# Windowed attention inside a two-layer MoE kernel: scores as 64x64 products in the visit of the values products, and a new order of each mixed step

## The chip, the core and the metric

The kernel runs on one core of a Trainium2 chip. The metric is the device time of one execution in microseconds, median of three. The core has five engines, each with its own in-order queue: TensorE (PE in the profile, its weight loads PEld), VectorE (DVE), ScalarE (ACT), GpSimd (POOL) and SyncE (SP, which here only issues DMAs). Matrix products land in PSUM, which has eight banks of 2 KB per partition; everything else lives in SBUF.

## What is computed

Three stages, one after the other. Attention over 4 batches, 8 heads, 576 positions and 64 channels, each query seeing the 64 positions that end at its own; then a dense MLP on 2304 tokens (512 to 2048 and back) with an activation called mish in the kernel; then a top-1 mixture of 8 experts.

```python
def _attn_ref(q, k, v):                       # [4, 8, 576, 64]
    scores = np.matmul(q, k.transpose(0, 1, 3, 2)) / np.sqrt(64)
    rel = pos[:, None] - pos[None, :]
    scores = np.where((rel >= 0) & (rel < 64), scores, -1000000000.0)
    attn = np.exp(scores - scores.max(-1, keepdims=True))
    return np.matmul(attn / (attn.sum(-1, keepdims=True) + 1e-09), v)

h = x @ w_in                                   # x: [2304, 512]
g = h * np.tanh(np.log1p(np.exp(h)))           # plain h above 20
x = g @ w_out
# each token: expert argmax(logits), out = prob * (relu(x @ w1[e]) @ w2[e])
```

## The kernel before

**Attention** goes by steps `a` of 64 queries (36 of them, two to a group `g`). A step's scores are four 128x128 tiles, one for each pair `c` of heads: rows are 2 heads x 64 queries, columns are 128 keys. `scores` (L150) first puts the mask into the bank by an identity product (L161, steps below `MASK_PE` = 26), then multiplies (L163) the keys by `qd`, a copy of the queries with zeros where the head and the channel half don't belong together; `qd` is cleared once (L107, L108) and filled by two DMAs per group (L139). `largest` (L172) takes the row maximum: below step 26 one reduction on VectorE (L178) and a scaling on GpSimd (L180), from step 26 on a fused mask-and-maximum on VectorE (L186). `exps` (L198) are four exponentials on ScalarE (L204), `inverse` and `scale` (L218, L228) normalise on GpSimd, `flip` (L235) transposes on TensorE (L241), `flipped` (L246) copies the transposed tile `t` to SBUF as `pt`, `values` (L249) multiplies with v (L257, eight 64x64 products), and `done` (L262) copies the result `o` out (L274) and, every second step, issues the store of x on ScalarE's queue (L277). `t` and `o` take turns in one PSUM bank, `s` has a bank of its own.

**Order.** Twelve attention steps run alone (`att_alone`, L1306). Then 28 mixed steps `i` follow, in which attention step and MLP step are woven together, with `na = 12 + i`. A mixed step is: 12 hidden products of MLP step `i` (L386 to L388, one weight load each, 512 columns), `att_a` (L1269), 12 output products of MLP step `i - 2` (L444 to L446; none in steps 0 and 1), `att_b` (L1291). So TensorE visits attention twice per step: scores of `na - 1` and flip of `na - 3` in `att_a`, values of `na - 3` in `att_b`. All engines run in exactly the order in which these Python functions issue.

**Woven in on VectorE and ScalarE**: mish in five ScalarE operations (L503 to L506, L514) and three VectorE operations (L508, L515, L516), the split of its result into a rounded part `g` and a rest (L522 on ScalarE, L523 on VectorE), and the conversion of 32 pieces of float64 weights, each three integer operations on VectorE (L330, L334, L338: the parts that `convert_start` counts), a cast on ScalarE (L356) and a subtraction on VectorE (L1252). The conversion is spread over the alone steps and the mixed steps 0 to 13, six or five parts a step (`CONV` = 3 in each half, one less in the second half of every third step).

After mixed step 27 the MLP goes on without attention, and then the routing and the experts.

Of the kernel before, what the change touches and what calls it, by code (L numbers as in the profile page):

```python
# [11 lines left out]
F32 = mybir.dt.float32  # L12
# [5 lines left out]
AF = mybir.ActivationFunctionType  # L18
# [23 lines left out]
PT_ACT = range(5, 28)  # L42
# [4 lines left out]
CONV = 3  # L47
# [42 lines left out]
class Attention:  # L90


    def __init__(self, nc, ctx, tc, qT, kT, v, x_dram, consts, spare, first_x):
        self.nc, self.qT, self.kT, self.v, self.x = nc, qT, kT, v, x_dram
        self.c = consts
# [3 lines left out]
        self.px = pool("att_x", 1)  # L99
# [3 lines left out]
        self.spare, self.first_x = spare, first_x  # L103
        self.qd = []
        for i in range(2):
            t = self.pq.tile([P, KD, 2, BLK * 2], F32, name=f"qd{i}")
            nc.vector.memset(t[0:64, :, 1], 0.0)  # L107
            nc.vector.memset(t[64:128, :, 0], 0.0)  # L108
            self.qd.append(t)
# [19 lines left out]
        self.kt, self.v_in, self.held = {}, {}, None  # L129
        self.s, self.p, self.t, self.o = {}, {}, {}, {}  # L130

    def load(self, g):
        nc = self.nc
        qd = self.qd[g % 2]
# [15 lines left out]
    def scores(self, a):  # L150
        nc = self.nc
        g, j = divmod(a, 2)
        if a % 2 and a < PRE:
            s = self.spare.tile([P, KD, P], F32, name="s_acc", tag="acc1")
        else:
            s = self.ps.tile([P, KD, P], F32, name="s")
        masked = a < MASK_PE
        if masked:
            mask = self.c["mask0_b"] if a % (S // BLK) == 0 else self.c["mask_b"]
            mask = mask.unsqueeze(1).broadcast_to([P, KD, P])  # L160
            nc.tensor.matmul(s, self.eye, mask, start=True, stop=False)  # L161
        for c in range(KD):
            nc.tensor.matmul(  # L163
                s[:, c, :],
                self.qd[g % 2][:, c].rearrange("p h (q j) -> p j (h q)", j=2)[:, j],
                self.kt[g][:, c, j * BLK : j * BLK + P],
                start=not masked,
                stop=not masked or c == KD - 1,
            )
        self.s[a] = s  # L170

    def largest(self, a, scaled_by=None):  # L172

        nc = self.nc
        s = self.s.pop(a)
        mx = self.pp.tile([P, KD], F32, name="mx")
        if a < MASK_PE:
            nc.vector.tensor_reduce(out=mx, in_=s, op=ALU.max, axis=AX.X)  # L178
            by = scaled_by or nc.gpsimd
            by.tensor_scalar(mx, mx, -1.0 / math.sqrt(HD), None, ALU.mult)  # L180
            self.p[a] = s, mx, 1.0 / math.sqrt(HD)
            return
        p = self.pp.tile([P, KD, P], F32, name="p")
        mask = self.c["mask0"] if a % (S // BLK) == 0 else self.c["mask"]
        for c in range(KD):
            nc.vector.tensor_tensor_reduce(  # L186
                out=p[:, c, :],
                in0=s[:, c, :],
                in1=mask,
                scale=-1.0 / math.sqrt(HD),  # L190
                scalar=3.0e38,
                op0=ALU.add,
                op1=ALU.min,
                accum_out=mx[:, c : c + 1],
            )
        self.p[a] = p, mx, -1.0

    def exps(self, a, alone=False):  # L198
# [4 lines left out]
        for c in range(KD):  # L203
            nc.scalar.activation(  # L204
                p[:, c, :],
                s[:, c, :],
# [26 lines left out]
    def flip(self, a):  # L233
        nc = self.nc
        p, _ = self.p.pop(a)  # L235
        if a < PRE - LT:
# [11 lines left out]

    def values(self, a):  # L249
# [3 lines left out]
        o = self.ps.tile([P, KD, BLK], F32, name="o", tag="to")  # L253
        for c in range(KD):
            for hh in (slice(0, 64), slice(64, 128)):
                d = slice(c * P + hh.start, c * P + hh.stop)
                nc.tensor.matmul(  # L257
                    o[hh, c, :], self.v_in[g][j][:, d], pt[:, c, hh], start=True, stop=True
                )
        self.o[a] = o  # L260

    def done(self, a):  # L262
# [11 lines left out]
        nc.scalar.copy(xs[:, :, j * BLK : (j + 1) * BLK], o)  # L274
# [23 lines left out]
class Rounds:  # L298
# [199 lines left out]
    def mish_a(self, h):  # L498

        nc = self.nc  # L500
        y = self.m_pool.tile([P, 2 * G], F32, name="y")
        r = self.m1_pool.tile([P, 2 * G], F32, name="r")
        nc.scalar.activation(y, h, AF.Tanh, scale=0.5)  # L503
        nc.scalar.activation(y, y, AF.Square, scale=-0.5, bias=self.c["half"][:, 0:1])  # L504
        nc.scalar.activation(r, y, AF.Exp, scale=SEED_B)
        nc.scalar.activation(r, r, AF.Copy, scale=SEED_A, bias=SEED_C)  # L506
        p = self.m1_pool.tile([P, 2 * G], F32, name="pq")
        nc.vector.scalar_tensor_tensor(p, y, 1.0, r, ALU.add, ALU.mult)  # L508
        return y, r, p, h

    def mish_b(self, y, r, p, h):
# [4 lines left out]
        nc.vector.scalar_tensor_tensor(y, p, -0.5, h, ALU.add, ALU.mult)  # L516
# [667 lines left out]
def tile_kernel(tc, a):  # L1184
    nc = tc.nc
    with ExitStack() as ctx:
# [22 lines left out]
        with tc.manual_schedule():  # L1209
# [4 lines left out]
            A = Attention(nc, att_ctx, tc, a["qT"], a["kT"], a["v"], a["x"], c, R.acc_ps, R.first_x)  # L1214
# [32 lines left out]

            def convert_end():
                def low():
                    while low_parts:  # L1250
                        key, args = low_parts.pop(0)
                        nc.vector.tensor_tensor(*args)  # L1252
                        ready.add(key)

                low()
# [488 lines left out]
```

## Time and profile before

| | |
|---|---|
| median of 3 runs | 722.13 us (721.99 to 722.43) |
| the profiled execution, its own time | 722.25 us |
| its span, first to last instruction | 720.5 us |
| TensorE busy | 699.2 us, 97% |
| VectorE busy | 539.2 us, 75% |
| ScalarE busy | 475.0 us, 66% |
| GpSimd busy | 152.2 us, 21% |
| chain that ended last | PE 81%, DVE 7%, ACT 4%, DMA 3%, issue 3% |

The span is what the trace covers; 1.75 us of the execution's own time lie around it. "Busy" is time with at least one instruction under way, over the whole span. The chain is the sequence of waits and instructions followed back from the last one. A matmul's duration is from its start to its end in the pipeline; what one costs in a row of them is the distance from its start to the next start. Products on float32 leave two records each (the mask and the 512-column products one).

### The profile page before, as it was taken

The numbers are of one execution on the slowest core, as the hardware profiler recorded it, in microseconds if no ns is written. First come the engines' busy times: TensorE is split into PE (matmuls) and PEld (weight loads), VectorE is DVE, ScalarE is ACT, GpSimd is POOL, SyncE is SP. The second block draws the span as 40 slices with busy tenths as digits, with TensorE's granted clock in tenths as the row PEclk, the third lists the DMA queues.
The fourth block names the chain that finished last, engine by engine and source line by source line (L and its number), as shares of the span: only waits on it lengthen the run. The fifth ranks groups of instructions, "written<-read, shape, count | busy, mean of one in ns | idle before, by whom it ended". The sixth has DMA issues, their size and how long they took to land.

```text
span 720.5 us, 11849 instructions
## 1 busy us (share of the span) xinstructions
PE 699.2 (97%) x4061; PEld 581.2 (81%) x4061; DVE 539.2 (75%) x1349; ACT 475.0 (66%) x1021; POOL 152.2 (21%) x290
## 2 busy tenths in 40 slices
PE   6879999999999999999999999999999999999996
PEld 5668877888888888888888888998888888888885
DVE  4889998976555479999999998699898754333361
ACT  4989888899777678776787677777454023342382
POOL 5753233332322010101101011401012305010031
PEclk9999999999999999999999999999999999999999
DMA  8996666752231332000000000732144604322340
GB/s 262 300 264 212 220 203 226 220 164 82 81 96 29 106 102 89 30 1 30 31 1 30 1 31 15 249 118 88 60 146 164 217 0 140 125 95 97 117 177 33
DMA packets 48615, 83.76 MB, mean 116 GB/s; under 512 B 3937, under 2 KB 23393, under 8 KB 48418
## 3 DMA queue, kind: packets, MB, share of 16 engines
q1 hardware_dynamic: 36578, 64.40, 28.7%
q0 software_dynamic: 4432, 14.46, 5.6%
q10 hardware_dynamic: 7536, 4.06, 2.0%
q8 instruction: 34, 0.56, 0.3%
q14 instruction: 35, 0.29, 0.1%
HBM read 69.78 MB, written 13.19 MB: 115 GB/s over the span
## 4 chain that ended last, share of the span: by engine, by line
PE 81%; DVE 7%; ACT 4%; DMA 3%; issue 3%; POOL 0%; SPq 0%; POOLq 0%; ACTq 0%
PE acc L444 11%; PE acc L446 11%; PE acc L445 11%; PE h L386 11%; PE h L388 11%; PE h L387 11%; PE s L163 3%; DMA qd<-qT 2%; PE o L257 2%; ACT p L204 1%; PE t L241 1%; PE h L374 1%; PE h L373 1%; PE h L370 1%; DVE cv L338 1%
## 5 line engine op out<-in xcount | busy, mean ns | idle before, releaser
L444 PE MATMUL acc<-w,g 128*128 128x512 f32 x256 | 102.8, 401 | 0.0
L653 DVE CUSTOM_DVE_ANT_0 junk<-row,wg 128x512 bf16<-128x512 f32 x144 | 99.1, 689 | 2.6
L446 PE MATMUL acc<-w,g 128*128 128x512 f32 x256 | 100.1, 391 | 0.0
L445 PE MATMUL acc<-w,g 128*128 128x512 f32 x256 | 99.8, 390 | 0.0
L530 ACT ACTIVATE g<-h 128x512 fp32r<-128x512 f32 x32 | 19.1, 598 | 112.0 <-PE h L388 111.2
L503 ACT ACTIVATE y<-h 128x512 f32<-128x512 f32 x72 | 43.0, 598 | 56.0 <-PE h L388 48.7
L231 POOL TENSOR_SCALAR p<-p,r 128x128 f32<-128x128 f32 x144 | 65.8, 473 | 65.5 <-DVE r L224 62.4
L386 PE MATMUL h<-xw,w 128*128 128x512 f32 x192 | 76.3, 398 | 0.0
L388 PE MATMUL h<-xw,w 128*128 128x512 f32 x192 | 75.0, 391 | 0.0
L387 PE MATMUL h<-xw,w 128*128 128x512 f32 x192 | 74.9, 390 | 0.0
L732 POOL DMA_INDIRECT xs_dram<-row,posi x18 | 20.0, 1111 | 228.2 <-DVE pq L515 83.7
L508 DVE SCALAR_TENSOR_TENSOR pq<-y,r 128x512 f32<-128x512 f32 x72 | 49.6, 689 | 24.3 <-ACT r L506 20.2
L514 ACT ACTIVATE pq<-pq,mid 128x512 f32<-128x512 f32 x72 | 52.4, 727 | 17.3 <-DVE pq L508 12.5
L531 DVE SCALAR_TENSOR_TENSOR g<-h,g 128x512 fp32r<-128x512 f32 x32 | 22.1, 690 | 55.0 <-ACT g L530 51.8
L523 DVE TENSOR_TENSOR g<-y,g 128x512 fp32r<-128x512 f32 x72 | 49.5, 687 | 17.8 <-ACT g L522 17.8
L515 DVE SCALAR_TENSOR_TENSOR pq<-pq,r 128x512 f32<-128x512 f32 x72 | 50.1, 696 | 13.4 <-ACT pq L514 11.5
L446 PEld LDWEIGHTS acc<-w,g 128*128 128x128 f32 x256 | 48.1, 188 | 10.6
L445 PEld LDWEIGHTS acc<-w,g 128*128 128x128 f32 x256 | 48.3, 189 | 9.2
L444 PEld LDWEIGHTS acc<-w,g 128*128 128x128 f32 x256 | 48.2, 188 | 9.0
L504 ACT ACTIVATE y<-y,half 128x512 f32<-128x512 f32 x72 | 52.2, 725 | 2.3
L516 DVE SCALAR_TENSOR_TENSOR y<-pq,h 128x512 f32<-128x512 f32 x72 | 49.5, 687 | 2.9
L444 PE MATMUL acc<-ew,g 128*128 128x512 f32 x128 | 50.8, 397 | 0.0
(296 smaller groups left out, 1782.4 us busy)
## 6 DMA issues: line engine op xcount, KB each, us to landing
s<-e_w SPq DMA_DIRECT2D x20, 1024.0 KB, 6.1
v<-v SPq DMA_DIRECT2D x36, 256.0 KB, 4.1
raw<-w_in SPq DMA_DIRECT2D x16, 512.0 KB, 5.0
raw<-w_out SPq DMA_DIRECT2D x16, 512.0 KB, 4.1
kt<-kT SPq DMA_DIRECT2D x17, 384.0 KB, 5.5
qd<-qT SPq DMA_DIRECT2D x36, 128.0 KB, 5.2
x_dram<-xs ACTq DMA_DIRECT2D x14, 256.0 KB, 3.2
xraw<-x_dram SPq DMA_DIRECT2D x10, 256.0 KB, 3.5
```

The lines of the kernel that those rows point to most:

```text
L231: nc.gpsimd.tensor_scalar(p[:, c, :], p[:, c, :], r[:, c : c + 1], 0.0, ALU.mult, ALU.add)
L386: nc.tensor.matmul(h, w[:, 0, k, fs], xh, start=(k == 0), stop=False)
L387: nc.tensor.matmul(h, w[:, 0, k, fs], xl, start=False, stop=False)
L388: nc.tensor.matmul(h, w[:, 1, k, fs], xh, start=False, stop=(k == KD - 1))
L444: nc.tensor.matmul(acc[c], gc[:, 0], w[:, 0, f], start=first, stop=False)
L445: nc.tensor.matmul(acc[c], gc[:, 0], w[:, 1, f], start=False, stop=False)
L446: nc.tensor.matmul(acc[c], gc[:, 1], w[:, 0, f], start=False, stop=last)
L504: nc.scalar.activation(y, y, AF.Square, scale=-0.5, bias=self.c["half"][:, 0:1])
L508: nc.vector.scalar_tensor_tensor(p, y, 1.0, r, ALU.add, ALU.mult)
L514: nc.scalar.activation(p, p, AF.Square, bias=self.c["mid"][:, 0:1])
L515: nc.vector.scalar_tensor_tensor(p, p, 0.75, r, ALU.add, ALU.mult)
L653: nc.vector.tensor_tensor_reduce(out=junk, in0=rows[c][:, 0:D], in1=self.wg[:, e], scale=1.0, scalar=0.0, op0=ALU.mult, op1=ALU.add, accum ...
```

## The change

- The queries are loaded as they are (`qt`, one DMA per group, 64 channels of one head of a pair on the lower and of the other on the upper 64 partitions), without zeros and without the clearing. Scores become eight products per step of 64 channels, 64 queries and 128 keys, ordered so that four successive ones use the four 64x64 quarters of the array; the mask becomes four products of 64x256. The row halves write to different banks: half 0 to the bank `xo` that `o` also uses (`s0`, columns 256 to 511), half 1 to the bank `s` (`s1`).
- In the mixed steps the scores of `na` (not of `na - 1`) are issued directly before the values of `na - 3`, so `att_a`'s visit keeps only the flip.
- `t`, `o` and one half of the scores now share one bank, so the flip must wait until the maximum, the exponentials (steps below 26) and the copy of `o` have read `xo`. Readers of `xo` on different engines are made to wait for one another (`one_at_a_time`).
- The maximum is two reductions, one for each bank, and its scaling in the mixed steps goes from GpSimd to VectorE (`shift`).
- Two tables, `ORDER_A` and `ORDER_B`, set each mixed step's order; mish is cut into parts that they name. The conversion parts are 6, 2, 5 and 3 in steps 0 to 3, six in each of steps 4 to 13, and the last three in step 14.
- The x tile `xs` gets a second buffer, and mixed step 0 copies `pt` on VectorE.

```diff
-PT_ACT = range(5, 28)
+PT_ACT = *range(5, 12), *range(13, 28)
-CONV = 3
+ORDER_A = {
...
+    None: ("done", "max 0", "high", "conv 1", "nm", "low", "conv 1", "scale", "y1", "conv 1", "y2", "fetch", "exps", "flip"),
+}
...
+for i in range(3):
+    n = 3
+    ORDER_B[i] = ("tanh", "pt", "mish", "high", "conv 1", "low", "conv 1", "pq", "conv 1", "scores", "max 1 next", "values", "g")
...
-        self.px = pool("att_x", 1)
+        self.px = pool("att_x", 2)
...
-        for hh in range(2):
-            hs = slice(64 * hh, 64 * hh + 64)
-            nc.sync.dma_start(qd[hs, :, hh], self.qT[g, hs])
+        self.qt[g] = self.pin.tile([P, KD, 2, BLK], F32, name="qt")
+        nc.sync.dma_start(self.qt[g], self.qT[g])
...
+        if a < PRE:
+            s0 = self.spare.tile([P, KD, P], F32, name="s0", tag="acc1")[:, 0:2]
+            if j:
+                s1 = self.spare_h.tile([P, KD, P], F32, name="s1", tag="h")[:, 0:2]
+            else:
+                s1 = self.ps.tile([P, KD, P], F32, name="s")[:, 0:2]
         else:
-            s = self.ps.tile([P, KD, P], F32, name="s")
+            s0 = self.xo[:, 2:4]
+            s1 = self.ps.tile([P, KD, P], F32, name="s")[:, 0:2]
+        s = s0, s1
         masked = a < MASK_PE
+        tiles = [(r, slice(64 * r, 64 * r + 64), h, slice(64 * h, 64 * h + 64))
+                 for h in range(2) for r in range(2)]
         if masked:
             mask = self.c["mask0_b"] if a % (S // BLK) == 0 else self.c["mask_b"]
-            mask = mask.unsqueeze(1).broadcast_to([P, KD, P])
-            nc.tensor.matmul(s, self.eye, mask, start=True, stop=False)
-        for c in range(KD):
-            nc.tensor.matmul(
-                s[:, c, :],
-                self.qd[g % 2][:, c].rearrange("p h (q j) -> p j (h q)", j=2)[:, j],
-                self.kt[g][:, c, j * BLK : j * BLK + P],
...
+            for r, rs, h, hs in tiles:
+                m = mask[rs].unsqueeze(1).broadcast_to([BLK, 2, P])
+                nc.tensor.matmul(s[r][hs], self.eye[rs, rs], m, start=True, stop=False)
+        for i in range(2):
+            for r, rs, h, hs in tiles:
+                c = 2 * i + h
+                nc.tensor.matmul(
+                    s[r][hs, i, :],
+                    self.qt[g][rs, c, j],
+                    self.kt[g][rs, c, j * BLK : j * BLK + P],
...
+    def room(self):
+        self.xo = self.ps.tile([P, KD, P], F32, name="xo", tag="to")
...
-        o = self.ps.tile([P, KD, BLK], F32, name="o", tag="to")
+        o = self.xo[:, 0:2].rearrange("p a (b q) -> p (a b) q", q=BLK)
...
+        self.one_at_a_time(a + LT, last)
...
+                    elif what == "scores":
+                        A.room()
+                        A.on(na) and A.scores(na)
```

**TensorE, a masked mixed step.** Before, from the last hidden products to the first output product: the first visit of the step (`eye` is the identity, `mask_b` the mask in bf16, x4 stands for four products in a row).

```order
L388 MATMUL h<-xh,w_1150 128x512
L161 LDWEIGHTS eye
L161 MATMUL s<-mask_b,eye 128x512
L163 MATMUL s<-kt,qd_126 128x128 x4
L241 MATMUL t<-ident,p 128x128 x4
L444 MATMUL acc_880<-w_1248,g 128x512
```

After, the same place and, behind the output products, the second visit, where before stood only the values products (L257).

```order
L450 MATMUL h<-xh,w_1388 128x512
L294 MATMUL t<-ident,p 128x128 x4
L506 MATMUL acc_995<-w_1496,g 128x512
...
L181 LDWEIGHTS eye
L181 MATMUL xo<-mask_b,eye 64x256
L181 LDWEIGHTS eye
L181 MATMUL s<-mask_b,eye 64x256
...
L185 MATMUL xo<-kt,qt 64x128
L185 MATMUL s<-kt,qt 64x128
...
L314 MATMUL xo<-pt,v_1516 64x64 x8
L448 MATMUL h<-xh,w_1604 128x512
```

The first visit has lost mask and scores; the second has gained four mask products and eight score products in front of the eight values products.

**ScalarE, the same kind of step.** Before, from the copy of `o` (L274) of one step to that of the next: the exponentials (L204) stand behind the mish of the step, and nothing on TensorE but the next scores waits for them.

```order
L274 COPY xs<-o 128x4x64
L356 CAST w_1050<-cv 128x512
L514 ACTIVATE pq<-pq,mid 128x512
L246 COPY pt<-t 128x512
L356 CAST w_1050<-cv 128x512
L503 ACTIVATE y<-h 128x512
L504 ACTIVATE y<-y,half 128x512
L505 ACTIVATE r<-y 128x512
L506 ACTIVATE r<-r 128x512
L204 ACTIVATE p,sm<-s,mx 128x128 x4
L522 CAST g<-y 128x512
```

After, over the same stretch:

```order
L336 COPY xs<-xo 128x4x64
L418 CAST w_1604<-cv 128x512
L581 ACTIVATE pq<-pq,mid 128x512
L257 ACTIVATE p,sm<-xo,mx 128x128 x2
L257 ACTIVATE p,sm<-s,mx 128x128 x2
L563 ACTIVATE y<-h 128x512
L299 COPY pt<-t 128x512
L569 ACTIVATE y<-y,half 128x512
L570 ACTIVATE r<-y 128x512
L571 ACTIVATE r<-r 128x512
L418 CAST w_1604<-cv 128x512
L591 CAST g<-y 128x512
```

The exponentials have moved ahead of the mish and of the copy `pt`; the two that read `xo` now stand before the flip of the same step.

**VectorE, one masked step with six conversion parts.** Before, a whole step from one maximum to the next (the conversion is L334, L338, L330 and L1252):

```order
L178 TENSOR_REDUCE mx<-s 128x4
L1252 TENSOR_TENSOR w_950<-cv,w_950 128x512
L334 SCALAR_TENSOR_TENSOR cv<-raw_850,cv 128x512
L338 SCALAR_TENSOR_TENSOR cv<-raw_850,cv 128x512
L330 TENSOR_SCALAR cv<-raw_904 128x512
L508 SCALAR_TENSOR_TENSOR pq<-y,r 128x512
L523 TENSOR_TENSOR g<-y,g 128x512
...
L224 RECIPROCAL r<-r 128x4
L515 SCALAR_TENSOR_TENSOR pq<-pq,r 128x512
L516 SCALAR_TENSOR_TENSOR y<-pq,h 128x512
```

After, the first two thirds of one:

```order
L221 TENSOR_REDUCE mx<-s 128x2
L592 TENSOR_TENSOR g<-y,g 128x512
L221 TENSOR_REDUCE mx<-xo 128x2
L392 TENSOR_SCALAR cv<-raw_1559 128x512
L246 TENSOR_SCALAR mx<-mx 128x4
L1326 TENSOR_TENSOR w_1604<-cv,w_1604 128x512
L396 SCALAR_TENSOR_TENSOR cv<-raw_1559,cv 128x512
L277 RECIPROCAL r<-r 128x4
L582 SCALAR_TENSOR_TENSOR pq<-pq,r 128x512
L400 SCALAR_TENSOR_TENSOR cv<-raw_1559,cv 128x512
L585 SCALAR_TENSOR_TENSOR y<-pq,h 128x512
```

The reduction is cut in two, the scaling (L246) is new here, and operations that feed each other (L396 and L400, L582 and L585) no longer stand next to each other.

## Rows read from the trace of the kernel before

**Rows 1.** The page: busy us, share of the span, instructions; and the chain by engine.
```profile
PE 699.2 (97%) x4061; PEld 581.2 (81%) x4061; DVE 539.2 (75%) x1349; ACT 475.0 (66%) x1021; POOL 152.2 (21%) x290
PE 81%; DVE 7%; ACT 4%; DMA 3%; issue 3%; POOL 0%; SPq 0%; POOLq 0%; ACTq 0%
```
**Rows 2.** Stretches: us, busy us of each engine (instructions), PEclk, DMA share, GB/s.
```profile
40.73:68.28 27.55, 25.33 (x183) 20.28 (x180) 23.74 (x45) 24.25 (x61) 9.18 (x20) 1.00 0.78 232
68.28:148.07 79.79, 79.66 (x535) 63.90 (x531) 75.61 (x138) 69.90 (x180) 26.86 (x62) 1.00 0.70 223
148.07:246.55 98.48, 98.48 (x666) 80.72 (x662) 59.61 (x167) 77.93 (x200) 25.09 (x62) 1.00 0.26 73
225.31:233.01 7.70, 7.70 (x56) 6.36 (x52) 4.44 (x14) 5.63 (x16) 2.06 (x5) 1.00 0.00 0
233.01:239.78 6.77, 6.77 (x48) 5.37 (x44) 3.98 (x7) 4.28 (x8) 1.84 (x4) 1.00 0.16 41
```
**Rows 3.** Timeline of TensorE in a masked mixed step: start, us, engine, line, operation.
```profile
102.69 0.39 PE L388 MATMUL h<-xh,w 128*128 128x512 f32 x1
102.92 0.39 PE L161 MATMUL s<-mask_b,eye 128*128 128x512 bf16 x1
103.14 1.10 PE L163 MATMUL s<-kt,qd 128*128 128x128 f32 x8
104.08 0.60 PE L241 MATMUL t<-ident,p 128*128 128x128 f32 x4
...
106.85 0.39 PE L445 MATMUL acc<-w,g 128*128 128x512 f32 x1
107.08 0.39 PE L446 MATMUL acc<-w,g 128*128 128x512 f32 x1
107.39 0.69 PE L257 MATMUL o<-pt,v 128*64 128x64 f32 x16
108.01 0.50 PE L386 MATMUL h<-xh,w 128*128 128x512 f32 x1
108.34 0.39 PE L387 MATMUL h<-xl,w 128*128 128x512 f32 x1
```
**Rows 4.** Matmuls on the tile `fx`: ns min/median/max, first and last start us.
```profile
L1081 PE MATMUL t<-s,fx x64: 272/273/298, 650.4 to 652.1; 128*32 128x128 f32 x64
```
**Rows 5.** Timeline of VectorE, a step with six conversion parts.
```profile
139.34 0.68 DVE L178 TENSOR_REDUCE mx<-s 128x4 f32<-128x512 f32 x1
139.94 0.68 DVE L1252 TENSOR_TENSOR w<-cv,w 128x512 fp32r<-128x512 f32 x1
140.54 0.68 DVE L334 SCALAR_TENSOR_TENSOR cv<-raw,cv 128x512 int32<-128x512 int32 x1
141.26 0.69 DVE L338 SCALAR_TENSOR_TENSOR cv<-raw,cv 128x512 int32<-128x512 int32 x1
141.87 0.42 DVE L330 TENSOR_SCALAR cv<-raw 128x512 int32<-128x512 int32 x1
...
145.74 0.17 DVE L224 RECIPROCAL r<-r 128x4 f32<-128x4 f32 x1
145.83 0.66 DVE L515 SCALAR_TENSOR_TENSOR pq<-pq,r 128x512 f32<-128x512 f32 x1
146.53 0.69 DVE L516 SCALAR_TENSOR_TENSOR y<-pq,h 128x512 f32<-128x512 f32 x1
147.13 0.68 DVE L178 TENSOR_REDUCE mx<-s 128x4 f32<-128x512 f32 x1
```
**Rows 6.** Timeline of ScalarE, parts of one step.
```profile
107.03 0.59 ACT L503 ACTIVATE y<-h 128x512 f32<-128x512 f32 x1
...
111.49 0.39 ACT L274 COPY xs<-o 128x256 f32<-128x256 f32 x1
111.91 0.52 ACTq L277 DMA_DIRECT2D x_dram<-xs  x1
112.48 0.72 ACT L514 ACTIVATE pq<-pq,mid 128x512 f32<-128x512 f32 x1 [0.60 <-DVE g L523]
113.11 0.57 ACT L246 COPY pt<-t 128x512 f32<-128x512 f32 x1
113.58 0.62 ACT L356 CAST w<-cv 128x512 fp32r<-128x512 f32 x1
114.10 0.60 ACT L503 ACTIVATE y<-h 128x512 f32<-128x512 f32 x1
```
**Rows 7.** The chain of waits, alone steps: start, us, what.
```profile
1.55 4.69 DMA qd<-qT
...
11.54 5.14 DMA qd<-qT
...
21.34 7.70 DMA qd<-qT
...
35.32 1.42 ACT p L204 x8
```
**Rows 8.** Timeline of SP's queue: the loads of one group.
```profile
10.58 0.33 SPq L136 DMA_DIRECT2D kt<-kT  x1
10.95 1.19 SPq L139 DMA_DIRECT2D qd<-qT  x2
```

More of the change, by code (lines that the diff above doesn't have):

```diff
@@ L102, in __init__ @@
         self.ps = pool("att_ps", 1, space=PSUM)
[L103 to L109, printed above, removed]
+        self.spare, self.spare_h, self.first_x = spare, spare_h, first_x
         for name in ("mask", "mask0"):
@@ new lines, in scores, with one_at_a_time @@
+        for i in range(2):
[5 more added lines that the diff above has]
+                    self.kt[g][rs, c, j * BLK : j * BLK + P],
+                    start=not masked,
+                    stop=not masked or i == 1,
+                )
+        self.s[a] = s
+    def one_at_a_time(self, a, op):
+        for other in self.reads.get(a, ()):
+            if other.ins.engine != op.ins.engine:
+                self.tc.add_manual_dep(
+                    op.ins,
+                    other.ins.name,
+                    mybir.DependencyInfo(
+                        mybir.DependencyClass.Sync, mybir.DependencyReason.DATA
+                    ),
+                    reason="both read one bank",
+                )
+        if a >= PRE:
+            self.reads.setdefault(a, []).append(op)
@@ L180, in largest, with shift @@
+    def shift(self, a, by):
+        s, (mx, p) = self.s.pop(a), self.mx.pop(a)
+        if p is None:
             by.tensor_scalar(mx, mx, -1.0 / math.sqrt(HD), None, ALU.mult)
             self.p[a] = s, mx, 1.0 / math.sqrt(HD)
[L182 to L195, printed above, removed]
@@ L252, in values @@
         pt = self.t.pop(a)
-        o = self.ps.tile([P, KD, BLK], F32, name="o", tag="to")
+        o = self.xo[:, 0:2].rearrange("p a (b q) -> p (a b) q", q=BLK)
         for c in range(KD):
[L255 to L258, printed above, removed]
+            cs = slice(c % 2 * BLK, c % 2 * BLK + BLK)
+            for r in range(2):
+                lo = c * P + r * 64
+                last = nc.tensor.matmul(
+                    o[r * 64 : r * 64 + 64, c, :],
+                    self.v_in[g][j][:, lo : lo + 64],
+                    pt[:, 2 * r + c // 2, cs],
+                    start=True,
+                    stop=True,
                 )
+        self.one_at_a_time(a + LT, last)
         self.o[a] = o
@@ L1323, in att_alone @@
                     A.flipped(na - LT, pt_copy())
+                    A.room()
                     A.values(na - LT)
@@ L1479, in finish_split, with tanh, mish_rest @@
                     pend = None
+            def tanh():
+                at, part, h = started.pop(0)
+                half.append((at, R.mish_1(h)))
+            def mish_rest():
+                at, parts = half[-1]
+                R.mish_2(*parts)
             def start_mish():
                 nonlocal mish
-                if part in ("m", "w"):
-                    mish = R.mish_a(h)
+                if started and not half:
+                    at, part, h = started.pop(0)
+                    if part not in ("m", "w"):
+                        return
+                    half.append((at, R.mish_1(h)))
+                    mish_rest()
+                at, parts = half.pop(0)
+                mish = (at, *R.mish_p(*parts))
+            started, half = [], []
             def pull(at):
```

212 lines of the change are left out of this document (134 added, 78 removed).

## The prediction

> **What bounds the kernel now.** I read the page's busy times and chain first: TensorE is busy 97% of the span and holds 81% of the chain [rows 1], so elsewhere time is won only where TensorE waits or where its work shrinks. Next the stretches of the mixed part [rows 2], because the change ends there. From 68.28 to 148.07 (mixed steps 4 to 13) TensorE is busy 79.66 of 79.79 us, 7.98 a step; but VectorE has 75.61 in the same time and ScalarE 69.90, so behind TensorE two engines stand at 95% and 88%. From 148.07 to 246.55 (steps 14 to 26) TensorE is busy all the time and VectorE only 59.61 of 98.48. From 40.73 to 68.28 (steps 0 to 3) TensorE idles 2.2 of 27.55. PEclk is 1.00 in every stretch, the 2.4 GHz level. Then single steps [rows 2]: one with unmasked scores takes 7.70, one without scores 6.77. The difference, 0.93, agrees with the timeline, where the eight records of the scores run from 103.14 to 104.08 [rows 3], 0.94 or 0.1175 a record. The mask in front takes 0.22 (102.92 to 103.14).
>
> **The score products.** They go from 8 records to 16 (two a product), each with a quarter of the array and the same 128 columns moving. No row shows 64x64 tiles with 128 columns. The nearest on one side are the values products, 64 weight columns and two tiles side by side: 16 records from 107.39 to 108.01 [rows 3], 0.039 each. On the other side are products with 32 weight columns on four tiles and 128 moving columns: 64 records in 1.7 us [rows 4], 0.027 each, a quarter of the 0.1175 less its fixed part. Bounds: 0.43 us (16 x 0.027) and 1.88 (16 x 0.1175, no overlap at all). I take 0.039, because the weights are 64 columns wide as there: 0.62.
>
> **The mask**, four products of 256 columns: 0.11 if four run side by side (half the columns of the 0.22), 0.44 if one after the other. I take 0.20, a little above four records at 0.039.
>
> **Changes of tile shape.** Into the values products the start distance is 0.31 where 0.23 is the rule (107.08 to 107.39, against 106.85 to 107.08), and behind them 0.33 (108.01 to 108.34) [rows 3]: 0.08 and 0.10. The new visit has one such change more, from scores to values: 0.09. The Trainium skill (TensorEngine Tiling (Array Packing), Key Properties) says that changing the tiling mode, unlike changing the tile, drains TensorE. It speaks against the change; the two gaps agree with it, at under 0.1 us each. By it the sum holds this term, 24 x 0.09 = 2.2 us; without it the forecast would be that much lower.
>
> **TensorE's step** is then 6.77 + 0.09 + 0.62 = 7.48 with unmasked scores (7.70 now) and 7.68 with masked ones (7.98 now).
>
> **VectorE and ScalarE in steps 4 to 13.** A step with six conversion parts takes VectorE 7.79 without idling (139.34 to 147.13) [rows 5]. The new order removes the extra of dependent neighbours: 0.72 instead of 0.60 between L334 and L338 (140.54 to 141.26, against 139.94 to 140.54), twice, and 0.70 instead of 0.60 behind L515; together 0.34. It adds a second reduction's fixed part and the scaling, each like the reciprocal, whose start distance is 0.09 and duration 0.17: 0.18 to 0.34. So VectorE needs 7.63 to 7.79, as much as TensorE. ScalarE's cycle is 7.07 with one weight cast and one store of x (107.03 to 114.10) [rows 6]; a second cast adds 0.52 (113.58 to 114.10), and only every second step has the store, 0.57 with its wait (111.91 to 112.48): 7.0 and 7.6 in turn, 7.3 on average. TensorE and VectorE thus bind together; I take 7.75 a step, 0.07 above 7.68 for waits on each other. GpSimd loses the scaling, and at 27 of 80 us [rows 2] it covers what remains.
>
> **Sum by stage.**
> - Steps 14 to 26: 10 x 7.48 + 3 x 6.77 = 95.1 instead of 98.5 (there are now ten steps with unmasked scores and three without, where one masked, ten and two stand today): -3.4. VectorE has room.
> - Steps 4 to 13: 77.5 instead of 79.8: -2.3.
> - Steps 0 to 3: two without output products, 7.68 - 12 x 0.23 = 4.92, and two of 7.68: 25.2 instead of 27.55. Of today's 2.2 of idle I leave 0.9, since step 1's scores follow the exponentials of step 0's scores closely: -1.4. These steps issue 16 conversion parts instead of 23, so VectorE is not late here.
> - Alone steps: the loads of the queries are on the chain three times (4.69, 5.14 and 7.70) [rows 7], and later ScalarE's exponentials are. The products there are shorter but not on the chain for long. The bytes stay; SP issues one load where it issued two in 1.19 [rows 8], so a landing can come 0.6 earlier. Nothing to 3 x 0.6 = 1.8; I take -1.0. What v and the weights queue behind on SP also moves 0.6 ahead. Clearing `qd` goes for nothing, since the first products wait for its load until 6.23 [rows 7].
> - The second `xs` buffer and the `pt` copy of step 0: nothing, hidden by the hidden products around them; without that cover at most one copy, 0.6.
>
> Together -8.1. The profiled execution took 722.25, of which 720.5 are span, and stands 0.12 above the median of the runs: **714.1 us**. What is won in the mixed part stays won: TensorE is the bound behind it.
>
> **Rivals.**
> *VectorE keeps steps 4 to 13 where they are.* For it: 75.61 of 79.79 [rows 2], and two reductions and a scaling more. Against it: the neighbours pulled apart. The 2.3 of that stage is lost: 716.4.
>
> *The tiles overlap only in pairs*, so that the change does not do what it says: 0.0585 a record, 0.94 a step, the scores cost what they do now. Steps of 7.80 and 8.00; stages 0.2, -0.2, 0.2 and 1.0 won, 721.1. Break-even for the whole kernel is near 0.06 a record. Without any overlap the step grows by a further 0.94 in all 24 steps: about 743. Rows 3 and 4 speak against both. The Trainium skill (TensorE: Matmul & The Clock Gate, Back-to-back issue gap) gives about 81 ns for a sustained pair of weight load and 128-column matmul; by that, as an estimate, 16 records are 1.30 us and the kernel comes out near 730. The trace's 0.027 and 0.039 a record speak against that as a floor for small tiles.
>
> *The flip waits for the exponentials: slower.* Place: the flip of steps 2 to 13, which writes the bank that `o` and half of the scores still occupy. From the end of the values products it needs the copy of `o` (0.39), a half reduction (about 0.35), a conversion part (0.42), the scaling (0.17) and two exponentials (half of 1.42 [rows 7]): 2.0. On ScalarE the queue up to there is 0.39 + 0.52 + 0.63 + 0.71 = 2.25, with the store 2.8. TensorE arrives after 12 x 0.23 = 2.76. So it just fits, if ScalarE is free when the values products end. For the rival: today the copy of `o` starts at 111.49 [rows 6], 3.4 us after its products end near 108.08 [rows 3]. Against it: ScalarE's 7.3 fit into 7.68, and the copy now stands ahead of the long row. It decides from a wait of 8.1 / 12 = 0.68 a step; with ScalarE 1 us late the time is 714.1 + 12 = 726.
>
> **How the numbers follow.** Forecast 0.58; VectorE 0.17; pairs 0.09; less overlap than pairs 0.04; flip 0.12. Best case of the forecast: 0.43 for the scores, 0.11 for the mask, so 7.29 and 7.40, VectorE at 7.63: 5.3 + 3.5 + 3.0 + 1.8 = 13.6, 708.6. The upper end takes in the pairs, 721.1, and leaves out the 0.16 behind it; so the range is 708.6 to 721.1, the forecast's own about 708.6 to 718. This kernel can be told from no change at 0.2%, 1.4 us: faster is below 720.7, slower above 723.6. Forecast, VectorE and half of the pairs are faster, 0.80; the rest of the pairs and a mild flip wait the same, 0.05; slower 0.15.
>
> **What would show it.** The 16 score records taking 0.5 to 0.65 in the timeline and the step with unmasked scores near 7.5 show the tiles right; 0.9 or more shows pairs. Steps 4 to 13 near 7.75 with VectorE above 95% busy show the two engines level; near 8.0 with TensorE idle behind VectorE, the first rival. An idle of TensorE ahead of the flip, put down to ScalarE's L257, of over 0.6 a step shows the last. The forecast is wrong if any of the first three stages gives back what the others win, or if a gain appears behind 250 us, where the change touches nothing.

## The result, and the profile after

The changed kernel takes **715.49 us** (median of four runs, 713.89 to 717.07) beside 722.28 for the kernel before on the same chip (721.99 to 722.84): ratio 0.9905, 95% interval 0.9882 to 0.9928. The forecast was 714.1 us, with a range of 708.6 to 721.1. The profiled execution took 715.24, its span is 713.5 (720.5 before).

The page of the changed kernel, busy times and chain by engine, beside [rows 1]:

```profile
PE 686.7 (96%) x4427; PEld 561.1 (79%) x4427; DVE 538.4 (75%) x1386; ACT 472.5 (66%) x1020; POOL 166.8 (23%) x276
PE 71%; DVE 16%; ACT 7%; issue 3%; POOL 1%; ACTq 0%; POOLq 0%; DVEq 0%
```

TensorE is busy 12.5 us less, yet the span is only 7.0 shorter: 5.5 us have become idle time. VectorE's share of the chain went from 7% to 16%, and DMA left it. The stretches show where; these are mixed steps 0 to 3, 4 to 13, 14 to 26, and steps 6 to 13 again alone (columns as in [rows 2]):

```profile
38.80:66.59 27.79, 26.12 (x234) 20.04 (x232) 22.42 (x47) 24.59 (x68) 7.93 (x15) 0.96 0.55 186
66.59:144.07 77.48, 76.10 (x644) 57.87 (x640) 76.87 (x161) 69.46 (x182) 43.60 (x55) 1.00 0.74 235
144.07:239.02 94.95, 94.46 (x736) 73.85 (x732) 59.65 (x170) 75.54 (x191) 24.80 (x59) 1.00 0.26 80
82.80:144.07 61.27, 60.82 (x516) 46.29 (x512) 61.27 (x129) 55.19 (x144) 32.65 (x42) 1.00 0.74 237
```

| stage | before | after | change | forecast |
|---|---|---|---|---|
| alone steps, to the first hidden product | 40.73 | 38.80 | -1.93 | -1.0 |
| steps 0 to 3 | 27.55 | 27.79 | +0.24 | -1.4 |
| steps 4 to 13 | 79.79 | 77.48 | -2.31 | -2.3 |
| steps 14 to 26 | 98.48 | 94.95 | -3.53 | -3.4 |
| behind that | 473.95 | 474.48 | +0.53 | 0 |

The last row holds nothing that the change touches; over nine of the kernels below it lies between 473.8 and 475.0.

**The score visit**, TensorE's timeline of the changed kernel, a step with unmasked and one with masked scores (of each four that start together only the first is shown; compare [rows 3]):

```profile
180.28 0.39 PE L508 MATMUL acc<-w,g 128*128 128x512 f32 x1
180.60 0.32 PE L185 MATMUL xo<-kt,qt 64*64 64x128 f32 x1
...
180.76 0.27 PE L185 MATMUL xo<-kt,qt 64*64 64x128 f32 x1
...
180.87 0.27 PE L185 MATMUL xo<-kt,qt 64*64 64x128 f32 x1
...
180.97 0.27 PE L185 MATMUL xo<-kt,qt 64*64 64x128 f32 x1
...
181.19 0.63 PE L314 MATMUL xo<-pt,v 128*64 128x64 f32 x14
```

```profile
111.79 0.39 PE L508 MATMUL acc<-w,g 128*128 128x512 f32 x1
112.11 0.29 PE L181 MATMUL xo<-mask_b,eye 64*64 64x256 bf16 x1
...
112.24 0.27 PE L185 MATMUL xo<-kt,qt 64*64 64x128 f32 x1
...
112.78 0.69 PE L314 MATMUL xo<-pt,v 128*64 128x64 f32 x16
```

Four records start together every 0.105 us: 16 take 0.42, 0.026 each, the best case of the forecast. Each quarter thus needs nearly as long for its record as the whole array needed for one of as many columns (0.1175, from [rows 3]); the gain is that four run side by side. The mask takes 0.13 (112.11 to 112.24). The changes of shape cost 0.09 ahead of the visit (0.32 instead of 0.23), 0.05 more between the first four records and the second (0.16 instead of 0.105), and 0.1 ahead of the values products (0.22 from the last four); a step without scores has the first of these too, so some 0.17 is new by these rows, and 0.19 by the steps (7.38 - 6.77 - 0.42).

**What waits now.** TensorE's idle times in the last alone step and in mixed steps 2 to 4, and the TensorE clock around the first mixed step, from the timeline and from stretches of the changed kernel:

```profile
37.75 1.12 PE L314 MATMUL xo<-pt,v 128*64 128x64 f32 x16 [1.80 <-ACT r L268]
...
57.14 0.27 PE L181 MATMUL xo<-mask_b,eye 64*64 64x256 bf16 x1 [0.41 <-ACT pt L299]
...
62.02 0.63 PE L294 MATMUL t<-ident,p 128*128 128x128 f32 x4 [0.53 <-issue]
...
70.45 0.63 PE L294 MATMUL t<-ident,p 128*128 128x128 f32 x4 [0.83 <-POOL r L276]
```

```profile
38.00:39.00 1.00, 1.00 (x17) 0.88 (x16) 0.96 (x3) 0.10 (x1) 0.00 (x0) 0.50 0.90 332
...
40.00:41.00 1.00, 1.00 (x4) 0.81 (x3) 0.25 (x2) 1.00 (x8) 0.58 (x2) 0.50 0.87 193
41.00:42.00 1.00, 1.00 (x5) 0.77 (x5) 0.00 (x0) 0.50 (x3) 0.83 (x3) 0.94 0.94 355
```

The last idle ahead of mixed step 0 in the kernel before:

```profile
40.11 0.69 PE L257 MATMUL o<-pt,v 128*64 128x64 f32 x16 [0.83 <-ACT p L204]
```

After 1.80 us of idling TensorE goes on at a granted clock of 0.50, the 1.2 GHz level, until past 41 us; in the kernel before it idled 0.83 us there, and the clock stayed at 1.00 from 40.73 on [rows 2]. Ahead of that TensorE was busy 10.27 us of the 18 from 20 to 38 us, and 14.26 in the kernel before. Mixed step 0 takes 5.93 us. The waits of steps 2 to 4 are all for ScalarE, or for what ScalarE waits for. These rows of ScalarE, VectorE and GpSimd stand behind them:

```profile
54.41 2.19 ACT L418 CAST w<-cv 128x512 fp32r<-128x512 f32 x4
56.48 0.61 ACT L299 COPY pt<-t 128x512 f32<-128x512 f32 x1
...
60.49 0.52 ACTq L339 DMA_DIRECT2D x_dram<-xs  x1
61.11 0.37 ACT L257 ACTIVATE p<-xo,mx 128x128 f32<-128x128 f32 x1 [0.65 <-DVE g L592]
...
69.54 0.37 ACT L257 ACTIVATE p<-xo,mx 128x128 f32<-128x128 f32 x1 [0.96 <-DVE mx L246]
```

```profile
69.18 0.26 DVE L246 TENSOR_SCALAR mx<-mx 128x4 f32<-128x4 f32 x1
```

```profile
66.53 2.89 POOL L284 TENSOR_SCALAR p<-p,r 128x128 f32<-128x128 f32 x4 [6.78 <-DVE r L277]
```

In step 2 `pt` stands behind four weight casts. In step 3 the exponentials stand behind the store of x (ScalarE's 0.65 of "idle" is its own DMA issue of 0.52), and end at 61.9, just before the flip at 62.02. In step 4 they stand behind VectorE's scaling of the maximum and end on `xo` at 70.34, behind the GpSimd operation that the row of the flip names; GpSimd's multiplications had started late as well.

**Alone steps.** The chain of waits of the changed kernel, one alone step:

```profile
17.17 0.59 ACT pt L299
17.76 1.41 ACT p L257 x8
...
19.19 0.30 ACT r L268
19.49 0.26 ACT xh L330
19.75 0.52 ACT w L418
20.27 0.49 ACT pt L299
```

ScalarE goes round in 3.1 us without a gap; where [rows 7] had three loads of queries, the chain now has none.

### The profile page after: what moved, and what is told of

Its sections match the earlier page's. It is cut to its first block, busy times and chain, and to the rows that moved or that the text cites. A ratio compares the mean times of both kernels' runs of the same rounds, so it can differ in the third digit from the quotient of the medians.

```text
span 713.5 us, 12581 instructions
## 1 busy us (share of the span) xinstructions
PE 686.7 (96%) x4427; PEld 561.1 (79%) x4427; DVE 538.4 (75%) x1386; ACT 472.5 (66%) x1020; POOL 166.8 (23%) x276
## 4 chain that ended last, share of the span: by engine, by line
PE 71%; DVE 16%; ACT 7%; issue 3%; POOL 1%; ACTq 0%; POOLq 0%; DVEq 0%
PE acc L506 11%; PE acc L507 11%; PE acc L508 11%; PE h L448 11%; PE h L450 10%; PE h L449 10%; ACT p L257 3%; DVE junk L722 2%; DVE w L1326 2%; PE xo L314 2%; DVE pq L575 2%; DVE g L592 2%; DVE cv L400 2%; DVE cv L396 1%; DVE y L585 1%
## 5 line engine op out<-in xcount | busy, mean ns | idle before, releaser
L284 POOL TENSOR_SCALAR p<-p,r 128x128 f32<-128x128 f32 x144 | 87.9, 626 | 113.9 <-DVE r L277 74.0
L582 DVE SCALAR_TENSOR_TENSOR pq<-pq,r 128x512 f32<-128x512 f32 x72 | 49.4, 686 | 11.1 <-ACT pq L581 8.6
L585 DVE SCALAR_TENSOR_TENSOR y<-pq,h 128x512 f32<-128x512 f32 x72 | 49.4, 686 | 2.5
L448 PE MATMUL h<-ex,ew 128*128 128x512 f32 x128 | 50.3, 393 | 0.0
```

The lines of the kernel that those rows point to most:

```text
L284: nc.gpsimd.tensor_scalar(p[:, c, :], p[:, c, :], r[:, c : c + 1], 0.0, ALU.mult, ALU.add)
L448: nc.tensor.matmul(h, w[:, 0, k, fs], xh, start=(k == 0), stop=False)
L585: self.nc.vector.scalar_tensor_tensor(y, p, -0.5, h, ALU.add, ALU.mult)
```

## The experiments

The stages of all kernels (us, profiled executions; each ratio is to runs of the kernel before on the same chip):

| kernel | median us | ratio, 95% interval | step 0 starts | 0 to 3 | 4 to 13 | 14 to 26 |
|---|---|---|---|---|---|---|
| before | 722.28 | | 40.73 | 27.55 | 79.79 | 98.48 |
| changed | 715.49 | 0.9905 (0.9882 to 0.9928) | 38.80 | 27.79 | 77.48 | 94.95 |
| e1_whole_products | 721.79 | 1.0001 (0.9985 to 1.0017) | 39.49 | 27.11 | 79.74 | 97.40 |
| e2_warm | 714.61 | 0.9894 (0.9878 to 0.9911) | 38.89 | 26.74 | 77.50 | 94.96 |
| e3_same_quarter | 716.6, one run | | 39.11 | 28.48 | 77.52 | 95.05 |
| e4_scaling_gpsimd | 713.75 | 0.9889 (0.9868 to 0.9911) | 38.34 | 26.66 | 77.50 | 94.65 |
| e5_pt_on_vector | 714.24 | 0.9889 (0.9872 to 0.9905) | 39.06 | 26.59 | 77.91 | 94.78 |
| e6_less_conversion | see below | | 38.58 | 26.76 | 76.84 | 94.79 |
| e7_scale_early | 714.18 | 0.9891 (0.9874 to 0.9907) | 38.98 | 26.41 | 77.57 | 94.93 |
| e8_store_on_sync | 712.81 | 0.9862 (0.9839 to 0.9884) | 38.33 | 25.94 | 77.89 | 94.53 |
| e9_together | 712.33 | 0.9854 (0.9831 to 0.9876) | 38.35 | 26.16 | 77.19 | 94.58 |
| e10_less_conversion_store | see below | | 38.30 | 26.02 | 75.94 | 94.37 |
| e11_both_scalings | 712.14 | 0.9844 (0.9821 to 0.9867) | 38.51 | 26.27 | 76.97 | 94.56 |

**1. The new order without the small products in the mixed steps.** From step 12 on the scores are 128x128 products again, at the new place and in the new order; they have the bank `s` to themselves, the queries come with zeros in two loads and `xs` has one buffer, all as before.

```diff
         else:
-            s0 = self.xo[:, 2:4]
-            s1 = self.ps.tile([P, KD, P], F32, name="s")[:, 0:2]
+            return self.whole(a)
...
+    def whole(self, a):
...
+        for c in range(KD):
+            nc.tensor.matmul(
+                s[:, c, :],
+                self.qd[g % 2][:, c].rearrange("p h (q j) -> p j (h q)", j=2)[:, j],
+                self.kt[g][:, c, j * BLK : j * BLK + P],
```

> From attention step 12 on the scores are again four whole 128x128 products on zero-padded queries, all in the bank s, at the new place and in the new order; the queries are loaded by two DMAs per group as before, and xs has one buffer. Theory (the overlap of the small products pays): unmasked steps go from 7.38 us to 7.7 to 7.85, steps 14 to 26 from 95.0 to about 98, steps 4 to 13 from 77.5 to about 80, the kernel to 720 to 723. Rival (the new order alone pays, the products are free): these stages stay within 0.5 us of 77.5 and 95.0 and the kernel at 715 to 717. For the alone steps: if the single load is what won 1.9 us there, mixed step 0 begins near 40.5 again; if the shorter products did, near 39.

The median is that of the kernel before. In steps 4 to 13 the new order alone brings nothing: TensorE is busy throughout, 7.97 a step (7.98 before), so that its own products set the step. The chain of the alone steps has loads of queries in it again. The stretch of steps 4 to 13, and two rows of that chain:

```profile
66.60:146.34 79.74, 79.74 (x535) 64.89 (x531) 77.25 (x162) 69.53 (x182) 44.60 (x55) 1.00 0.73 229
```

```profile
1.55 4.60 DMA qd<-qT
...
14.45 7.16 DMA qd<-qT
```

So the small products are what shortens the mixed steps: 79.74 to 77.48 in steps 4 to 13, and 97.40 to 94.95 in steps 14 to 26. The other 1.08 of the 3.53 in steps 14 to 26 are won with whole products too, since one step more has no scores there. The profiled execution was the fastest of ten (720.20 to 725.29; mean granted clock 0.997 there and 0.990 in the slowest), so what its stages won is not in the median. Whether the small products would win as much in the old order, no run shows.

Mixed step 0 still starts 1.24 us earlier than before, with the small products only in the alone steps. The single load may be worth the other 0.69, but kernels with the same alone phase start step 0 up to 0.5 us apart (38.80 as changed, 38.34 in e4_scaling_gpsimd), so this part is uncertain.

**2. Does the order among the four quarters matter?**

```diff
-        for i in range(2):
-            for r, rs, h, hs in tiles:
+        for r, rs, h, hs in tiles:
+            for i in range(2):
```

> The eight score products go quarter by quarter, two successive products on the same quarter of the array, instead of changing the quarter with each product. Theory (the gain is the overlap of four quarters, and TensorE takes products in their order): the 16 records take 1.2 to 1.9 us instead of 0.44, unmasked steps 8.1 to 8.8, the kernel 735 to 746. Rival (the order among the products does not matter): 715 to 717.

Two successive products now use the same quarter, and the records still run in four streams. The timeline of this kernel: the first record of the first quarter and of the last, the first quarter's second record, and the end of the visit:

```profile
120.76 0.27 PE L185 MATMUL xo<-kt,qt 64*64 64x128 f32 x1
...
120.80 0.32 PE L185 MATMUL s<-kt,qt 64*64 64x128 f32 x1
120.87 0.27 PE L185 MATMUL xo<-kt,qt 64*64 64x128 f32 x1
...
121.37 0.34 PE L314 MATMUL xo<-pt,v 128*64 128x64 f32 x4
```

Steps with unmasked scores take 7.40 us (7.38 as changed). The theory is refuted and its rival met: the last quarter starts (120.80) before the first has come to its second record (120.87). Across quarters the starts did not keep to the order in which the kernel issues the products; the quarters overlap in this order too, and a no-overlap price can't be had this way.

**3. Is it the clock that makes step 0 long?** Four to seven products of 512 columns, whose result nobody reads, stand ahead of the values products of alone steps 6 to 11.

```diff
+WARM = {6: 4, 7: 4, 8: 4, 9: 4, 10: 4, 11: 7}
...
+                    warm(WARM.get(na, 0))
                     A.room()
                     A.values(na - LT)
```

> Four to seven idle mask products (identity by mask into a free bank, read by nobody) stand before the values products of alone steps 6 to 11, where TensorE waits. Theory (TensorE's clock fell to its lower level at 38 us because TensorE waited so long before): granted clock 1.00 from 30 to 45 us, mixed step 0 takes 4.8 to 5.1 us instead of 5.93, the kernel 714.0 to 714.6 and the runs lie closer together than the 3.2 us of now. Rival (the clock has nothing to do with it, or the added products delay the values products): step 0 as long as now, 715.3 to 717.

The stretch from 36 to 44 us of this kernel:

```profile
36.00:44.00 8.00, 7.70 (x96) 5.38 (x89) 6.21 (x15) 6.68 (x24) 3.85 (x8) 1.00 0.77 250
```

The granted clock is 1.00 (0.79 as changed), and step 0 takes 4.86 instead of 5.93. The four runs lie within 0.3 us, those of the changed kernel within 3.2, and there the longer the lower the mean granted clock: 713.89 at 0.998, 715.24 and 715.74 at 0.995, 717.07 at 0.990. The medians alone (0.9894 against 0.9905) would not show it.

**4. The scaling of the maximum back on GpSimd.**

```diff
-                        A.on(b) and A.shift(b, nc.vector)
+                        A.on(b) and A.shift(b, nc.gpsimd)
```

> The scaling of the maximum in the mixed steps goes back to GpSimd; nothing else changes. Theory (VectorE's load is what sets steps 4 to 13): VectorE sheds 0.09 to 0.17 us a step, steps 4 to 13 take 76 to 77 us instead of 77.5, the kernel 714 to 715. Rival (the path from the maximum to the exponentials sets the flip, so the longer hop to GpSimd, 0.6 us before, is paid): TensorE waits before the flip by 0.2 to 0.6 us a step, the kernel 717 to 721.

Steps 4 to 13 stay at 77.50, where 76 to 77 was expected. Inside, step 4 grows from 8.47 to 8.99, and steps 5 to 13 fall from 69.0 to 68.5 and now alternate, 7.73 and 7.48. That pattern is followed up in 5 and 7. The profiled span is 2.2 us shorter than as changed, but not by VectorE's load: 1.1 of it is step 0 (4.85 instead of 5.93) at a granted clock that stayed at 1.00, 0.46 lies in the alone steps and 0.34 behind step 26, where the edit changes nothing, and 0.30 in steps 14 to 26. TensorE idled the same 1.80 us ahead of step 0, after as little work (10.22 of the 18 us from 20 to 38): that does not lower the clock every time. In e3_same_quarter it did again, and step 0 took 6.44.

**5. Does VectorE bind steps 5 to 13?** Here the third integer operation of each conversion is left out in steps 4 to 13.

```diff
+        if not self.short:
+            nc.vector.scalar_tensor_tensor(
+                t, high, -0x40000000, t, ALU.bitwise_and, ALU.bitwise_or
+            )
```

> The kernel of e2_warm without the third integer operation of each weight conversion in mixed steps 4 to 13 (two a step of some 0.60 us each on VectorE; the weights converted there are wrong). Theory (VectorE binds steps 5 to 13: it is busy 61.27 of 61.27 us between 82.80 and 144.07 in the changed kernel, 7.66 a step, where TensorE alone would need 7.38 + 0.13 = 7.51): a step of 7.5 us, TensorE busy all the time, steps 4 to 13 at 75.5 to 76.3 instead of 77.5, VectorE at 87% or less. Rival 1 (TensorE or ScalarE binds there by itself, VectorE is only full because it fills its waits): 77.3 to 77.5, no change. Rival 2 (ScalarE is next, at 6.9 us a step plus waits): 76.5 to 77.

The whole time (794.03) says nothing, since tokens are routed by other values; the 80 us more lie behind mixed step 27. Steps 5 to 13 take 68.4 instead of 69.0: VectorE did bind, but the gain is small, since the steps now take 7.72 and 7.44 in turn. Steps 4 to 13, 76.84, lie where the second rival put them, ScalarE next. Timelines of TensorE and ScalarE of this kernel, a long step (104.15 to 111.85) and the flip of a short one:

```profile
106.78 0.39 PE L452 MATMUL h<-xh,w 128*128 128x512 f32 x1
107.27 0.63 PE L295 MATMUL t<-ident,p 128*128 128x128 f32 x4
...
114.48 0.39 PE L452 MATMUL h<-xh,w 128*128 128x512 f32 x1
114.71 0.49 PE L295 MATMUL t<-ident,p 128*128 128x128 f32 x3
```

```profile
104.27 0.37 ACT L337 COPY xs<-xo 128x256 f32<-128x256 f32 x1 [0.39 <-PE xo L315]
104.67 0.52 ACTq L340 DMA_DIRECT2D x_dram<-xs  x1
105.23 0.62 ACT L420 CAST w<-cv 128x512 fp32r<-128x512 f32 x1 [0.59 <-DVE mx L222]
...
106.39 0.35 ACT L258 ACTIVATE p<-xo,mx 128x128 f32<-128x128 f32 x1
...
106.98 0.19 ACT L258 ACTIVATION_READ_ACCUMULATOR p<-xo,mx 128x1 f32 x1
```

In the long step the flip starts 0.49 us behind the last hidden product, 0.10 after the second exponential has left `xo` (106.98 + 0.19). In the short one, without a store, it follows after 0.23. So the store of x, on ScalarE ahead of the exponentials, costs TensorE 0.26 every second step. The page counts no idle there, because the modelled ends of the products overlap.

**6. The waits of steps 2 to 4.** First `pt` of step 2 on VectorE (with the fillers of 3), then the scalings earlier as well.

```diff
-PT_ACT = *range(5, 12), *range(13, 28)
+PT_ACT = *range(5, 12), 13, *range(15, 28)
```

> The kernel of e2_warm, but mixed step 2 copies pt on VectorE. Theory (steps 2 to 4 are long because ScalarE is late: in step 2 the scores wait 0.41 us for pt, which stands behind four weight casts of 2.19 us, in step 3 the flip waits 0.53 us for exponentials that end 0.6 us later than they could): step 2 goes from 8.45 to about 8.0 us, step 3 from 8.13 to about 7.7, steps 0 to 3 from 26.7 to 25.8, steps 4 to 13 stay at 77.5; about 713.7 us beside 714.6 of e2_warm. Rival 1 (the copy on VectorE comes too late itself, since VectorE is as full): step 2 at 8.4 or more, no gain. Rival 2 (VectorE, which binds from step 4 on, is handed the 0.6 us as backlog): steps 0 to 3 shorter by up to 0.9 and steps 4 to 13 longer by the same, 714.6 us.

```diff
-    2: ("done", "exps", "conv 2", "y", "high", "scale", "fetch", "flip"),
+    2: ("done", "exps", "scale", "conv 2", "y", "high", "fetch", "flip"),
...
+    4: ("done", "max 0", "nm", "high", "conv 1", "low", "conv 1", "scale", "y1", "conv 1", "y2", "fetch", "exps", "flip"),
```

> The kernel of e5_pt_on_vector with three rows of the order changed: in mixed steps 2 and 3 the reciprocal and GpSimd's scaling stand right behind the exponentials, in step 4 the scaling of the maximum stands right behind the second reduction. Theory (the flip of step 4 waits 0.83 us because VectorE comes late to the scaling of the maximum, 69.18 us, and GpSimd starts its four multiplications only at 66.53 after 6.78 us of idling): step 4 at 7.7 to 8.0 us instead of 8.45, 0.5 to 0.8 us less than e5_pt_on_vector. Rival (VectorE's backlog sets step 4, whatever the order of its operations): step 4 at 8.3 to 8.5, or the gain of step 4 lost in steps 5 to 7, the same time as e5_pt_on_vector.

In the first, step 2 falls to 8.02 as expected, but steps 3 and 4 grow to 8.38 and 8.94: from the start of step 0 to that of step 5 it takes 35.53 us, 35.19 in e2_warm. In the second the three steps are 7.95, 8.27 and 8.54, and step 5 starts after 34.95. Only 0.24 us are won, less than expected: each wait that goes is followed by the next one. What sets the start of step 5 in the end stayed open.

**7. The store of x on SyncE** (with the fillers and GpSimd's scaling).

```diff
-            nc.scalar.dma_start(self.x[b, :, :, t * P : (t + 1) * P], xs)
+            (nc.sync if a >= PRE - LT else nc.scalar).dma_start(self.x[b, :, :, t * P : (t + 1) * P], xs)
```

> The changed kernel with the five fillers of e2_warm, the scaling of the maximum on GpSimd as in e4_scaling_gpsimd, and the store of x in the mixed steps issued by SyncE instead of ScalarE. Theory (with VectorE relieved, every second step is 7.7 instead of 7.45 us because ScalarE issues the store of x, 0.52 us, ahead of the exponentials and the flip then waits about 0.26 us for them): all steps 5 to 13 at 7.45 to 7.5 us, no interval of 0.49 us from the last hidden product to the flip, steps 4 to 13 at 75.8 to 76.3 instead of 77.5; step 3 about 0.4 us shorter as well, since its exponentials waited 0.65 us for the store; 712.3 to 713.3 us. Rival 1 (the longer steps come from something else that has a period of two, the loads of k and q or the start of a pair of output products): the 7.7 stay, no change. Rival 2 (SyncE, waiting for the copy of x, holds up the loads behind it): a wait on a load appears and the time is at or above that of e4_scaling_gpsimd, 713.8 us.

The alternation is gone, yet steps 5 to 13 still take 68.3 us, 7.59 each, with VectorE busy all of the last eight:

```profile
81.27:142.16 60.89, 60.85 (x516) 46.32 (x513) 60.89 (x121) 55.47 (x144) 33.47 (x48) 1.00 0.73 240
```

So the two limits stand at nearly the same height. Step 3 falls to 7.44 as expected; step 4 returns it (9.56). Steps 4 to 13 take 77.89 where 75.8 to 76.3 was expected, and the time met its range (712.3 to 713.3) by other stages. Together with the shorter conversion:

> The kernel of e6_less_conversion (two integer operations less a step on VectorE in mixed steps 4 to 13) with the store of x issued by SyncE. Steps 5 to 13 took 7.66 us as changed (VectorE full), 7.58 with VectorE relieved alone (7.72 and 7.44 in turn), 7.59 with the store moved and VectorE relieved by the scaling only. Theory (two limits of nearly the same height stand over TensorE's own 7.45: VectorE, and in every second step ScalarE with the store): with both away every step takes 7.43 to 7.47, steps 5 to 13 together 67.0 us, against 68.2 in e6_less_conversion. Rival (a third limit is close behind): 7.55 or more.

Steps 5 to 13 of this kernel (the whole time, 791.02, again says nothing):

```profile
73.30:140.26 66.96, 66.96 (x581) 52.76 (x577) 61.76 (x127) 62.15 (x162) 26.25 (x45) 1.00 0.72 243
```

They take nine times 7.44, as expected, with TensorE busy all the time. That is TensorE's own step with masked scores, and beside it both limits show: VectorE at 7.6 and, in every second step, ScalarE at 7.72.

**8. Together.**

> The kernel of e7_scale_early (fillers, pt of step 2 on VectorE, the earlier scalings) with the scaling of the maximum on GpSimd and the store of x on SyncE. If the gains add up: steps 0 to 3 at 26.0 to 26.4, steps 4 to 13 at 75.5 to 76.3, steps 14 to 26 at 94.6 to 95.0, 711.8 to 712.8 us. If the scaling on GpSimd comes later there than on VectorE (rival: GpSimd's four multiplications, 2.5 to 3.2 us, stand in front of it): step 4 at 8.5 to 9.0 and no better than e8_store_on_sync.

> The kernel of e9_together, but up to mixed step 4 VectorE scales the maximum, and GpSimd only from step 5 on. Expected: step 4 at 8.4 to 8.6 us instead of 8.86, steps 5 to 13 as in e9_together (68.3 us), 711.9 to 712.3 us. Rival (VectorE's backlog is carried into step 5): no difference from e9_together, 712.3 us.

The first has the fillers, the scalings of 6, GpSimd's scaling and the store on SyncE; in the second VectorE scales the maximum up to step 4. Both beat the changed kernel by some 3 us, 712.33 and 712.14. Steps 4 to 13 take 77.19 and 76.97, where 75.5 to 76.3 was expected of the first: its time met the range (711.8 to 712.8), the stage did not. Between them the difference is no more than the measurement can tell; step 4 is 8.65 instead of 8.86.

## Why the prediction was right, and where it was not

The sum of -8.1 came out as -7.0, near by some luck: the alone steps won 0.9 more than forecast, steps 0 to 3 missed by 1.6. (722.25 less 8.1 and 0.12 is 714.0, not 714.1; nothing hangs on it.)

**Steps 14 to 26**, -3.4 forecast, -3.53 measured: the right mechanism with two sizes off that partly cancel. The 16 records took 0.42 instead of 0.62, nearer to the products with 32 weight columns on four tiles [rows 4] than to the values products [rows 3] that I had chosen for their width, but of which only two run side by side. The Trainium skill (TensorE: Matmul & The Clock Gate, "Wait — 56ns, not 53.3ns?") says that starts never come closer than about 25 ns; the mean of 26 ns here agrees with that, and not with the 81 ns that the prediction weighed; but within a four the starts are shown 10 ns apart or less, so between quarters it was no floor. The changes of shape took 0.19 instead of 0.09. A step is 7.38 instead of 7.48, of which the first three steps of the stage gave some back (7.53, 7.94, 7.51).

**Steps 4 to 13**, -2.3 forecast, -2.31 measured, by another balance than I gave. TensorE needs 7.44, not 7.68, so that the two "bind together" was wrong. VectorE binds, at the lower end of the 7.63 to 7.79 that [rows 5] gave, and beside it, in every second step, ScalarE with the store: 7.72, where the prediction had 7.6 and then took the average of 7.3. Steps 5 to 13 take 7.67, below the 7.75 forecast, and step 4 takes 8.47: that the two add up to the forecast is luck. The first rival, VectorE keeping the old time, did not happen.

**Steps 0 to 3**, -1.4 forecast, +0.24 measured: **the step that failed**. "Two without output products, two of 7.68", 25.2, and "0.9 of idle" left out two things. Measured are 2.6 us above 25.2. Of these 1.05 are the clock (e2_warm: 27.79 to 26.74), which I had taken as 1.00 throughout because [rows 2] showed it so; but a TensorE with less work idled longer ahead of step 0 (1.80 instead of 0.83). The other 1.54 are waits: 0.38 in step 1 (5.30 instead of 4.92), the place for which the 0.9 was meant, and 1.22 in steps 2 and 3 (8.45 and 8.13 instead of 7.68), for which nothing was left and where ScalarE is late; step 0 at full clock gives 0.06 back. I had looked whether VectorE is late there, by its conversion parts, but not at ScalarE, busy 24.25 of 27.55 already before [rows 2].

**Alone steps**, -1.0 forecast, -1.93 measured. The loads did leave the chain, but 1.24 came with the loads put back (e1). I had put the shorter products at nothing, since they are "not on the chain for long"; the first scores alone run 1.06 us (from 5.44) where they ran 2.05 (from 6.37). How the 1.24 divides between them and the rest of the new alone steps, no run separates.

**The flip that waits for the exponentials**, the rival with slower: it is there, at 0.26 us in every second step when VectorE is out of the way, and at 0.53 and 0.83 in steps 3 and 4, on average over the twelve steps far below the 0.68 from which it would have decided. My count gave 2.76 for TensorE's arrival and 2.8 for ScalarE with the store; in e6_less_conversion TensorE could have come after 2.86 (104.15 to 106.78 and 0.23) and the flip started after 3.12. **Pairs** are refuted by the 0.105 between fours.

## What to carry to other kernels

Small tiles that fill the array together pay in full only where nothing else stands close to TensorE. Before counting the gain, work out every engine's step at the new height, step by step where steps differ, DMA issues on compute queues included: here VectorE and a 0.52 us store on ScalarE both lay within 0.3 us of TensorE. And shortening TensorE's work in a phase that another engine bounds lengthened its idle time here, which in some executions cost its clock at the start of the next phase.

## What the runs showed of the hardware

GpSimd's four multiplications by the reciprocal take twice as long where they now stand. Rows by group, first between 82 and 142 us before, then the same after, then after between 165 and 210 us, where no weights are converted:

```profile
L231 POOL TENSOR_SCALAR p<-p,r 128x128 f32<-128x128 f32 x32 | 13.3, 429 | 27.0 <-DVE r L224 27.0
```

```profile
L284 POOL TENSOR_SCALAR p<-p,r 128x128 f32<-128x128 f32 x33 | 28.6, 882 | 27.7 <-PE t L294 27.7
...
L284 POOL TENSOR_SCALAR p<-p,r 128x128 f32<-128x128 f32 x24 | 11.1, 477 | 29.3 <-DVE r L277 29.3
```

VectorE was nearly full in the first as well (56.07 of 60 us); what differs is which of its operations run beside. The Trainium skill (SBUF — State Buffer, SBUF: two separate sides) says that a VectorE operation with two inputs from SBUF and a GpSimd operation that reads SBUF lock one another out. The times go with it. Of VectorE's operations here, two of the conversion's three integer ones, its subtraction and the first two of mish have two such inputs; they ran beside 0.79 of the multiplications' time at 882 ns, 0.54 at 614 ns (e6_less_conversion) and 0.24 at 429 ns, where the reduction and the last operation of mish, which read PSUM, ran beside most of it. No run isolated it.

Four 64x64 quarters ran side by side in both orders tried of their products, each at 0.105 to 0.11 us per record of 128 columns.
